# Eight accumulator banks cut by hand from one tile instead of pool buffers, in an attention and feed-forward kernel

## Chip, cores, metric

The kernel runs on one core of a Trainium2 chip. The metric is the device time of one execution in microseconds (us). In the text PE is TensorE, DVE is VectorE, ACT is ScalarE, POOL is GpSimd and SP is SyncE, which here only issues transfers.

## What is computed

Causal attention with a decay term, and a feed-forward layer on its output. There are 64 heads (batch 8 by 8) of 576 positions and 64 columns; the feed-forward layer has 4608 rows, 512 columns in and out, and 2048 columns between.

```python
scores = scale * np.matmul(q, k.transpose(0, 1, 3, 2))
cum = np.cumsum(np.maximum(s, 0.0), axis=-1)
bias = -(cum[:, :, :, None] - cum[:, :, None, :])
scores = np.where(causal, -1000000000.0, scores + np.minimum(bias, 0.0))
attn = np.exp(scores - np.max(scores, axis=-1, keepdims=True))
attn = attn / (np.sum(attn, axis=-1, keepdims=True) + 1e-09)
x = np.matmul(attn, v)          # heads side by side: (4608, 512)
h = x @ w_in                    # (4608, 2048)
g = h * np.clip(h + 3.0, 0.0, 6.0) / 6.0
out = g @ w_out                 # (4608, 512)
```

## The kernel before

**Work and tiles.** Heads go in pairs p = 0 to 31. For a pair, q and k are brought into columns: for the first ten pairs by PE transposes (`transpose_group`, L247, two groups, evacuated by DVE in the copies of L262), for later pairs by a transposing DMA (`transpose_dma`, L229) out of a staging tile `xb`. POOL fills `xb` in `cast_columns` (L222, L225, L226), with decay columns that `decay_columns` (L201 on PE, L214 and L216 on DVE) makes once.

A head's scores stand in four banks (`scores_bank`, L291 on PE). Each bank goes through an exponential on ACT (L299) and a causal mask on POOL (L304). `attend` (L340) multiplies the result by the values, and DVE divides by the row sums (L350, L352). `x_transpose` puts the result into columns, by PE (L378, copied by DVE in L386) or by a transposing DMA (L370).

The feed-forward layer runs over blocks of 512 rows. `m1` (L423) makes one of 16 pieces of h, ACT takes the relu (L431) and DVE the product (L432); `m2` (L450) makes 128 rows of the output, evacuated by DVE (L459).

**Accumulator banks.** PSUM has eight banks of 128 partitions by 512 float32. A pool holds them under four tags: "S" with three buffers (scores, PE transposes of later pairs, decay columns, some m1 pieces at the end), "M" with two (m1, some m2, early transposes), "Y" with one, and "O" with one buffer of two banks. A request for a tile of a tag gets a buffer of it, and the first writer of the new tile waits for what used the old one.

**Order.** The order of all work is written out by hand. The scheduler is off (`manual_schedule`), so each engine runs its instructions in the order of the program; `weave` lays attention tasks between the feed-forward tasks. SP issues nearly all transfers, in one queue, in program order. What the framework adds are the semaphore waits.

Of the kernel before, what the change touches and what calls it, by code (L numbers as in the profile page):

```python
# [9 lines left out]
F32 = mybir.dt.float32  # L10
F16 = mybir.dt.float16
# [5 lines left out]
def kernel(  # L17
# [30 lines left out]

    cpool = ctx.enter_context(tc.tile_pool(name="consts", bufs=1))
    work = ctx.enter_context(tc.tile_pool(name="work", bufs=2))  # L50
    psum = ctx.enter_context(tc.tile_pool(name="psum", bufs=1, space=bass.MemoryType.PSUM))

    def bank():
        return psum.tile([128, 512], F32, tag="M", bufs=2, name="bank")
# [14 lines left out]
        name="xaug",  # L69
# [527 lines left out]
    def att_tasks(p):  # L597


        more = p + 1 < NP  # L600

        def loads():
            if p + 3 < NP:
                load_qk(p + 3, nc.sync)
                load_v(p + 3, nc.sync)
            if p < PTD - 1:
                cast_qk(p + 1)

        def casts():
            if more:  # L610
                cast_v(p + 1)
            if PTD <= p + 2 < NP:
                cast_columns(p + 2)
                transpose_dma(p + 2)

        tr = [[], []]
        if p + 1 < min(NP, PTD):
            tr = [[(lambda: transpose_group(p + 1, 0), 640)],
                  [(lambda: transpose_group(p + 1, 1), 512)]]
        late = [(lambda: attend(2 * p - 1), 1200)] if p > 8 else []  # L620
        back = []
        if p > 8:
            back = [(lambda: x_transpose(p - 1), 0 if by_dma(p - 1) else 640)]
        a = [(loads, 0)]
        if p <= PXD:
            a += scores(2 * p) + tr[0] + late
            a += scores(2 * p + 1) + [(casts, 0)] + tr[1] + back
        else:
            s0, s1 = scores(2 * p), scores(2 * p + 1)
            a = late + (back + a if by_dma(p - 1) else a + s0[:2] + back)  # L630
            a += (s0 if by_dma(p - 1) else s0[2:]) + tr[0]
            a += s1 + [(casts, 0)] + tr[1]
        return a, [(lambda: attend(2 * p), 1200)]

    att_of = [[]]
    for p in range(8, NP):
        a, c = att_tasks(p)
# [124 lines left out]
```

The softmax here doesn't subtract the row's maximum and nothing guards it: scores larger than these inputs give would overflow.

## Time and profile before

| what | value |
|---|---|
| time, median of 3 runs | 375.04 us (374.9 to 375.15) |
| span of the profiled execution | 374.1 us |
| PE, busy | 354.2 us |
| ACT, busy | 209.8 us |
| DVE, busy | 190.4 us |
| POOL, busy | 149.1 us |
| HBM, over the span | 126 GB/s |

The busy time of an engine is a sum over the whole span, and matmuls overlap in the pipeline, so PE's share is not its distance from the peak. In the page's groups, the columns are: line, engine, operation, output and inputs, shape, count; then busy time and mean duration in ns; then the idle time of the engine just before these instructions and what ended it. A row of a timeline has start and length in us, engine, line, operation and count, and in brackets the idle time before it with its releaser. A row of a table of stretches has the stretch, its length, the busy time of PE, weight loads, DVE, ACT and POOL with their counts, the granted PE clock, the DMA share and GB/s.

### The profile page before, as it was taken

How to read it: one execution, taken by the hardware profiler on the slowest of the kernel's cores; microseconds unless marked ns; L12 is line 12 of the kernel's file. 1: busy time of each engine (PE TensorE's matmuls, PEld its weight loads, DVE VectorE, ACT ScalarE, POOL GpSimd, SP SyncE). 2: the span in 40 equal slices, each digit the busy share in tenths (PEclk: the TensorE clock that was granted, in tenths of full speed). 3: DMA queues.
4: the chain of work that ended last, by engine and by line, in shares of the span. 5: the costliest groups of instructions: out<-in, count | busy, mean ns of one | idle time of the engine just before them, and what ended most of it. 6: DMA issues, size and time to landing. Idle time of an engine off the chain costs nothing.

```text
span 374.1 us, 7656 instructions
## 1 busy us (share of the span) xinstructions
PE 354.2 (95%) x2805; PEld 220.5 (59%) x2805; DVE 190.4 (51%) x331; ACT 209.8 (56%) x405; POOL 149.1 (40%) x378
## 2 busy tenths in 40 slices
PE   6878879999999899999999999999999999999996
PEld 2455556556666566566656665666566655555544
DVE  5765856566642355345534553455345535554431
ACT  4464764336885677467746774677467714553310
POOL 5673344454666344444444444444444300000000
PEclk9999999999999999999999999999999999999999
DMA  9689999938899999899999989899995200011012
GB/s 162 137 155 210 205 218 204 237 108 180 157 190 197 231 172 235 188 232 198 198 208 222 206 177 234 194 196 180 213 194 112 56 31 28 28 39 46 28 58 84
DMA packets 184670, 59.36 MB, mean 159 GB/s; under 512 B 177856, under 2 KB 178336, under 8 KB 184632
## 3 DMA queue, kind: packets, MB, share of 16 engines
q1 hardware_dynamic: 182392, 54.28, 70.2%
q0 software_dynamic: 1680, 4.27, 6.4%
q8 instruction: 22, 0.36, 0.4%
q10 hardware_dynamic: 560, 0.32, 0.3%
q14 instruction: 16, 0.13, 0.1%
HBM read 37.49 MB, written 9.62 MB: 126 GB/s over the span
## 4 chain that ended last, share of the span: by engine, by line
PE 81%; DVE 5%; ACT 4%; DMA 4%; issue 2%; POOL 1%; SPq 1%; ACTq 0%; POOLq 0%
PE bank L423 26%; PE po L450 23%; PE S L291 10%; PE bank L450 7%; PE O L340 6%; PE bankS L423 4%; ACT Pm L299 3%; DMA qkT<-xb 2%; ACT trl L431 1%; DMA qkf<-in_k_dram 1%; DVE gT L432 1%; DVE qkT L262 1%; PE bank L490 1%; PE bankY L423 1%; DMA s_sb<-in_s_dram 1%
## 5 line engine op out<-in xcount | busy, mean ns | idle before, releaser
L299 ACT ACTIVATE Pm<-S 128x384 f16<-128x384 f32 (+2 forms) x256 | 115.5, 508 | 58.4 <-PE S L291 56.6
L432 DVE SCALAR_TENSOR_TENSOR gT<-trl,bank 128x512 f16<-128x512 f32 x123 | 84.5, 687 | 102.2 <-ACT trl L431 101.9
L304 POOL TENSOR_SCALAR_AFFINE_SELECT Pm<-Pm 128x128 f16<-128x128 f16 (+2 forms) x256 | 79.4, 312 | 132.7 <-ACT Pm L299 122.7
L431 ACT ACTIVATE trl<-bank,bias 128x512 f32<-128x512 f32 x123 | 85.2, 692 | 77.3 <-PE bank L423 75.5
L423 PE MATMUL bank<-xT,w_in 128*128 128x512 f16 x492 | 126.4, 382 | 0.7
L450 PE MATMUL po<-w_out_sb,gT 128*128 128x512 f16 x416 | 104.3, 379 | 0.0
L423 PEld LDWEIGHTS <-w_in 128*128 128x128 f16 x576 | 78.5, 146 | 33.3 <-issue 2.4
L450 PEld LDWEIGHTS <-gT 128*128 128x128 f16 x560 | 50.7, 98 | 46.8 <-issue 0.3
L291 PE MATMUL S<-qkT 128*128 128x320 f16 (+4 forms) x448 | 70.2, 261 | 6.8 <-ACT Pm L299 3.4
L291 PEld LDWEIGHTS <-qkT 128*128 128x128 f16 x448 | 41.0, 98 | 36.4 <-issue 3.6
L340 PEld LDWEIGHTS <-Pm 128*128 128x128 f16 x960 | 38.3, 97 | 13.4 <-POOL Pm L304 1.8
L340 PE MATMUL O<-v_h,Pm 128*128 128x65 f16 x960 | 40.8, 193 | 1.5 <-POOL Pm L304 1.3
L450 PE MATMUL bank<-w_out_sb,gT 128*128 128x512 f16 x144 | 35.8, 379 | 0.0
L352 DVE TENSOR_TENSOR xs<-O,r 128x640 f16<-128x640 f32 x32 | 26.4, 824 | 1.1
L459 DVE TENSOR_SCALAR osb<-po 128x512 f32<-128x512 f32 x26 | 17.9, 688 | 15.2 <-PE po L450 14.9
L222 POOL CAST xb<-qkf 128x1152 f16<-128x1152 f32 x22 | 25.3, 1150 | 0.0
L238 POOL CAST v_h<-v_f 128x640 f16<-128x640 f32 x28 | 20.2, 720 | 3.0 <-DMA v_f<-in_v_dram 3.0
L459 DVE TENSOR_SCALAR osb<-bank 128x512 f32<-128x512 f32 x9 | 6.2, 691 | 23.2 <-PE bank L450 23.2
L176 POOL CAST t<-qkf 128x1152 f16<-128x1152 f32 x10 | 11.5, 1154 | 13.7 <-DMA qkf<-in_k_dram 13.7
L423 PE MATMUL bankS<-xT,w_in 128*128 128x512 f16 x64 | 16.4, 379 | 0.0
L431 ACT ACTIVATE trl<-bankS,bias 128x512 f32<-128x512 f32 x16 | 11.0, 688 | 8.0 <-PE bankS L423 8.0
L432 DVE SCALAR_TENSOR_TENSOR gT<-trl,bankS 128x512 f16<-128x512 f32 x16 | 11.0, 688 | 6.8 <-ACT trl L431 6.8
(55 smaller groups left out, 130.8 us busy)
## 6 DMA issues: line engine op xcount, KB each, us to landing
qkf<-in_q_dram SPq DMA_DIRECT2D x32, 288.0 KB, 4.2
qkf<-in_k_dram SPq DMA_DIRECT2D x32, 288.0 KB, 4.3
out_dram<-osb SPq DMA_DIRECT2D x35, 256.0 KB, 2.4
v_f<-in_v_dram SPq DMA_DIRECT2D x64, 128.0 KB, 4.0
w_in<-in_moe_w_in_dram POOLq DMA_DIRECT2D x2, 1024.0 KB, 12.8
w_out_sb<-in_moe_w_out_dram POOLq DMA_DIRECT2D x4, 512.0 KB, 7.3
v_f<-in_v_dram SPq DMA_DIRECT2D x32, 32.0 KB, 2.7
qkT<-xb SPq DMA_TRANSPOSE x22, 4.9
```

The source lines that it names most:

```text
L222: nc.gpsimd.tensor_copy(out=x.rearrange("p (i t) c -> p t i c", i=2)[:, :, :, 0:D], in_=qk_f.pop(p))
L238: copy(out=v_h[:, sl, :, :, 0:D], in_=v_f[:, sl])
L291: nc.tensor.matmul(out=S[:, c:c + hi - lo], lhsT=kT[:, sl, off + 128 * kt:off + 128 * (kt + 1)], rhs=qT[:, sl, off + lo:off + hi], start=( ...
L299: nc.scalar.activation(out=P[:, p0:p0 + n], in_=S[:, 0:n], func=AF.Exp, scale=0.125, bias=0.0)
L304: nc.gpsimd.affine_select(out=view, in_=view, pattern=pattern, compare_op=ALU.is_ge, fill=0.0, base=0, channel_multiplier=-1,)
L340: nc.tensor.matmul(out=O[:, hh, qt * VW:qt * VW + D + 1], lhsT=P[:, c:c + 128], rhs=v_h[:, sl, hh, kt, 0:D + 1], start=(qt == 0), stop=(qt ...
L352: nc.vector.tensor_tensor(out=xs.rearrange("p t h d -> p h t d"), in0=Ov[:, :, :, 0:D], in1=r.to_broadcast([128, 2, 5, D]), op=ALU.mult,)
L423: nc.tensor.matmul(out=ph, lhsT=w_in_t[f // 8][:, kc, f % 8, :], rhs=xT[:, kc, n * 512:(n + 1) * 512], start=(kc == 0), stop=(kc == KC - 1),)
L431: nc.scalar.activation(out=trl, in_=ph, func=AF.Relu, bias=bias3[:, 0:1], scale=1.0)
L432: nc.vector.scalar_tensor_tensor(out=gT[n][:, f, :], in0=trl, scalar=6.0, in1=ph, op0=ALU.min, op1=ALU.mult)
L450: nc.tensor.matmul(out=po, lhsT=gT[n][:, f, t4 * 128:(t4 + 1) * 128], rhs=w_out_sb[:, f, :], start=(f == 0), stop=(f == NF - 1),)
L459: nc.vector.tensor_scalar_mul(out=osb, in0=po, scalar1=1.0 / 6.0)
```

## The change

The pool now holds one tile, `PS`, of all eight banks. A small class cuts tiles from it by hand: a counter for each tag, and the bank is the counter modulo the number of banks of the tag, so the banks of a tag are used strictly in turn. The kernel's calls stay as they are; `psum` is now this class. The framework sees one tile that lives throughout, and derives the waits from accesses to the same bank in it, instead of from the release and reuse of a buffer. It is meant to give the author the choice of the bank and to leave out the bookkeeping of buffers that are handed back.

```diff
-    psum = ctx.enter_context(tc.tile_pool(name="psum", bufs=1, space=bass.MemoryType.PSUM))
+    pspool = ctx.enter_context(tc.tile_pool(name="psum", bufs=1, space=bass.MemoryType.PSUM))
+    PS = pspool.tile([128, 8, 512], F32, tag="PS", name="PS")
+
+    class Banks:
+        first = {"S": (0, 3), "M": (3, 2), "Y": (5, 1), "O": (6, 2)}
+        n = {}
+
+        def tile(self, shape, dtype, tag, bufs=1, name=None):
+            b0, k = self.first[tag]
+            i = self.n.get(tag, 0)
+            self.n[tag] = i + 1
+            if tag == "O":
+                return PS[:, 6:8, :]
+            b = b0 + i % k
+            t = PS[:, b, :]
+            if dtype == F16:
+                t = t.bitcast(F16)
+            if len(shape) == 2:
+                return t[:, 0:shape[1]]
+            return t[:, 0:shape[1] * shape[2]].rearrange("p (a b) -> p a b", a=shape[1])
+
+    psum = Banks()
```

## The prediction

> **What bounds the kernel now.** I read the page first: engine shares, then the chain of waits, then stretches of the span, then the timeline at the places where the two programs differ.
>
> ```profile
> PE 354.2 (95%) x2805; PEld 220.5 (59%) x2805; DVE 190.4 (51%) x331; ACT 209.8 (56%) x405; POOL 149.1 (40%) x378
> ...
> PE 81%; DVE 5%; ACT 4%; DMA 4%; issue 2%; POOL 1%; SPq 1%; ACTq 0%; POOLq 0%
> ...
> L299 ACT ACTIVATE Pm<-S 128x384 f16<-128x384 f32 (+2 forms) x256 | 115.5, 508 | 58.4 <-PE S L291 56.6
> ...
> L291 PE MATMUL S<-qkT 128*128 128x320 f16 (+4 forms) x448 | 70.2, 261 | 6.8 <-ACT Pm L299 3.4
> ```
>
> TensorE (PE) is the bound; the score matmuls of L291 are the row with most idle time in front. A delay counts only if PE cannot make it up. From 127 to 309 us PE shows 181.36 us of 182 busy, so whatever is lost earlier is kept to the end. Before 127 there is one long link that is not PE:
>
> ```profile
> 92.00:93.00 1.00, 1.00 (x19) 0.76 (x18) 0.99 (x3) 0.54 (x1) 1.00 (x3) 1.00 0.00 0
> 93.00:94.00 1.00, 1.00 (x7) 0.68 (x6) 0.85 (x3) 0.32 (x2) 1.00 (x2) 1.00 0.00 0
> 94.00:95.00 1.00, 1.00 (x6) 0.64 (x6) 0.97 (x3) 0.91 (x3) 0.38 (x4) 1.00 0.00 0
> ...
> 100.00:110.00 10.00, 9.76 (x87) 6.58 (x88) 6.38 (x11) 7.68 (x16) 6.64 (x16) 1.00 1.09 195
> ...
> 94.37 2.81 SPq L229 DMA_TRANSPOSE qkT<-xb  x1
> ...
> 125.32 0.56 PE L291 MATMUL S<-qkT 128*128 128x256 f16 x4 [1.03 <-DMA qkT<-xb]
> ```
>
> The second number from the right is the DMA share: zero from 92 to 95, because SyncE's queue holds its next transfer, the transposing DMA of L229, until GpSimd (POOL) has filled xb. From 96 on the DMA engines are saturated (1.08 to 1.20) until 125.27, when the transpose issued at 119.11 lands and PE, idle for 1.03 us, goes on. So the start of that DMA burst at 94.37 sets the rest of the kernel: late by x there is late by x at the end.
>
> **What the Trainium skill says.** "TensorE: Matmul & The Clock Gate", The mechanism: matmuls are "strict FIFO" in start and end, so a matmul that waits for an older matmul of PE waits for nothing new. The trace agrees: L291 matmuls carrying such a wait start 0.216 us after a 512-column matmul and 0.056 us after a 128-column one, as matmuls without one do. "PSUM — Partial Sum Buffer", PSUM bank collisions raise a hardware error: accesses are to be guarded by semaphore per bank (and quadrant), so either kernel must make PE wait for the last reader of the same bank; what can change is which bank comes next. "Perfetto Trace Analysis", Identifying Dependency Chains: an instruction that waits on several engines may get a separate semaphore instruction ahead of it; the trace has such rows, 51 ns (median) on PE for L291 and 28 ns on SyncE for L229.
>
> **The change, part by part.** I listed both built programs, each instruction with what it waits for, and matched them to the trace by position. The order on all five engines is the same, instruction for instruction. The waits differ.
>
> (1) Self-waits of PE: 74 matmuls lose a wait for an older matmul, which a returned pool buffer brought along; 6 of them now wait for VectorE (DVE) instead, a wait that stood on their weight load before. By the pitches above the removed ones cost 0. This edit is hidden by PE's own order.
>
> (2) Six weight loads lose a DVE wait, to the matmul behind them. Where it ends last (10.44, 55.98, 72.62, 73.51 us) the weight load may now run ahead. The matmuls stood at most 0.01 us behind those loads and 0.05 us behind the release, as matmuls that wait themselves do, so I take 0; the upper bound is one load, 98 ns by its row, at four places, 0.4 us.
>
> (3) Added waits: 21 exponentials of L299 also wait for DVE, and 11 DVE copies (L262, L386) for ScalarE (ACT): the previous reader of their bank. The matmul that filled the bank already waited for that reader, so these are past when reached. Semaphore instructions go from 393 to 388 on ACT and from 57 to 68 on DVE; 11 times 28 to 51 ns is 0.3 to 0.6 us of DVE, busy for 51%, beside its wait for PE: 0 on the path. L431's waits for the older reader of trl become self-waits of ACT or go: 0.
>
> (4) Which bank comes next. The pool has not handed out the three "S" banks strictly in turn; the hand-written rotation does. At four places the next score tile gets a bank that DVE still holds.
>
> Near 46.9 us both releases (46.53, 46.63) come before the matmul starts (46.96): 0.
>
> Near 56.4 us:
>
> ```profile
> 55.98 0.72 PE L291 MATMUL S<-qkT 128*128 128x192 f16 x4 [0.55 <-DVE qkT L262]
> 57.07 0.30 PE L291 MATMUL S<-qkT 128*128 128x320 f16 x1 [0.36 <-DVE xT L386]
> ```
>
> The third bank of this head (matmuls at 56.38 and 56.52) waited for an exponential that ended at 56.33, and the fourth, at 57.07, for the xT copy of L386 that ended at 57.02. Now the third waits for the copy and the fourth for the exponential. All three matmuls start after 57.02 instead of one: the two moved ones, 0.14 and 0.03 us by their pitches, come in front of the fourth. Cost 0.17 us. Behind it stand an m1 group and the next scores; nothing up to 76 is set by DMA, so PE keeps the delay.
>
> Near 76.5 us three banks were read by the decay copies of L214. Before: the second bank started at 76.46 (exponential, 76.41), the third at 76.67, the fourth at 77.00 (copies, 76.95). Now the second may start at 76.20, the third waits for 76.95, the fourth follows it by 0.17: 77.17 against 77.00. Cost 0.17 us; the second bank's earlier start helps nobody, as ACT's next exponential still stands behind the third.
>
> Near 89.5 us, the costly one:
>
> ```profile
> 89.22 0.57 PE L291 MATMUL S<-qkT 128*128 128x192 f16 x4
> 89.63 1.06 PE L423 MATMUL bank<-xT,w_in 128*128 128x512 f16 x4
> 90.53 0.30 PE L291 MATMUL S<-qkT 128*128 128x320 f16 x1
> ...
> 89.35 0.98 DVE L262 COPY qkT<-pT 64x640 f16<-64x640 f16 x2
> ```
>
> The third bank's matmul, at 89.47 inside the first row, waited for an exponential that ended at 89.42. Now it waits for the second of the two copies in the last row, which ends at 90.33. It starts at 90.38, 0.91 us late, with nothing for PE to do meanwhile. Queued behind it on PE are the m1 group (row two) and the fourth bank (row three, now about 91.44). ACT's relu on that group, which is ahead of the fourth bank's exponential, was held by ACT's own queue for some 0.1 us, so the exponential at 91.42 slips by about 0.8. POOL's mask waits for it, then v_h, then the three copies into xb, back to back from 91.95 to 94.35, then the L229 transpose: 94.37 becomes 95.17. The saturated burst behind it passes that on to 125.32. Cost 0.8 us.
>
> Sum: 0.17 + 0.17 + 0.8 = 1.14 us. 375.04 + 1.14 = 376.2. In the steady part after 127 the pool and the rotation ask for the same readers, so nothing is added.
>
> **The rivals.** *Swallowed:* the saturated burst has some spare, or PE's short idle spots between 57 and 89 (0.3 us at 72.6, 0.4 us at 79.0) take up the 0.34 of the first two places and a part of the third. For it: PE arrives at 125.32 with 1.03 us in hand. Against: that slack is ahead of a DMA that is itself late, and DMA is empty, not busy, just before the burst. Taking half of the 1.14: 375.6. *Faster:* the self-waits or the earlier weight loads are worth more than I read. 0.4 us from the loads, and if each of the 74 waits cost even 0.02, 1.5 more, less the delay of 1.14: 374.3. Against: the pitch of the matmuls that carry them. *Much slower:* the later burst meets other traffic, and the transposes issued later in it stop PE at further score groups; twice the third place, 0.34 + 1.6: 377.0.
>
> **How the numbers follow.** Forecast 0.66, swallowed 0.17, faster 0.12, much slower 0.05. The 0.2% bound is 0.75 us, so same is 374.29 to 375.79. The forecast at 376.2 has a spread of about 0.3, so a little of it falls into same; some of the faster cases lie within 0.75. Faster 0.10, same 0.20, slower 0.70. Range 374.8 to 376.9: it takes in swallowed and most of the forecast's upper side, and leaves out the larger gain and the larger loss.
>
> **What would show it.** Right: in the profile after, an idle spot of about 0.6 us or more ahead of an L291 matmul near 90.4 us (plus 0.3), released by the qkT copy; the first L229 transpose near 95.5; PE going on after the DMA wait near 126.4; the stretch from there to the end as long as before, 248.8 us. At 57 and 77 us the waits for DVE are longer and those for ACT gone. Steps (1) to (3) are wrong if matmul pitches at the former self-waits fall below 0.216 or 0.056, or if DVE waits grow at copies. The prediction falls if the transpose starts at 94.4 as before, if PE waits less at 125, or if the part after 127 changes its length.

## The result, and the profile after

The changed kernel takes 376.71 us (median; 376.35 to 377.39), the kernel before 375.0 us (374.9 to 375.15). The ratio is 1.0043, 95% interval 1.0029 to 1.0057: slower by 1.6 us (1.1 to 2.1). The changed kernel's source has 21 lines more ahead of the body, so L291 is L312 here, L423 is L444, L262 is L283, L386 is L407, L214 is L235 and L229 is L250; all accumulator tiles are named PS.

First the page: the sums hardly moved.

```profile
PE 354.7 (95%) x2805; PEld 220.6 (59%) x2805; DVE 190.5 (51%) x331; ACT 209.8 (56%) x405; POOL 148.5 (40%) x378
...
L312 PE MATMUL PS<-qkT 128*128 128x320 f16 (+4 forms) x448 | 70.2, 261 | 7.9 <-ACT Pm L320 2.8
```

The busy time of the score matmuls is the same 70.2 us; the idle time in front of them grew from 6.8 to 7.9. A loss of this kind is not in any engine's share. Which waits end that idle time is told by PE's waits between 50 and 130 us. The kernel before:

```profile
PE S L291 <- ACT Pm L299: 1.3, 4, 0.6
...
PE S L291 <- DMA qkT<-xb: 1.0, 1, 1.0
PE S L291 <- DVE qkT L262: 0.5, 1, 0.5
...
PE S L291 <- DVE xT L386: 0.4, 1, 0.4
```

and the changed kernel, in the same stretch (total us, times, longest):

```profile
PE PS L312 <- DVE qkT L283: 1.3, 2, 0.8
...
PE PS L312 <- DVE dec L235: 0.8, 2, 0.4
PE PS L312 <- DVE xT L407: 0.7, 1, 0.7
PE PS L312 <- ACT Pm L320: 0.6, 3, 0.3
PE PS L312 <- DMA qkT<-xb: 0.6, 1, 0.6
```

Score matmuls wait 2.8 us for DVE instead of 0.9, and 0.6 for ACT instead of 1.3. The timeline of the changed kernel's PE has the three places, in order, then the matmul behind the DMA wait; the last row is SP's queue.

```profile
57.06 0.46 PE L312 MATMUL PS<-qkT 128*128 128x320 f16 x3 [0.71 <-DVE xT L407]
...
76.34 0.38 PE L312 MATMUL PS<-qkT 128*128 128x192 f16 x2 [0.42 <-DVE dec L235]
77.14 0.46 PE L312 MATMUL PS<-qkT 128*128 128x320 f16 x3 [0.42 <-DVE dec L235]
...
90.69 0.33 PE L312 MATMUL PS<-qkT 128*128 128x320 f16 x2 [0.79 <-DVE qkT L283]
90.85 1.06 PE L444 MATMUL PS<-xT,w_in 128*128 128x512 f16 x4
91.75 0.30 PE L312 MATMUL PS<-qkT 128*128 128x320 f16 x1
...
126.12 0.56 PE L312 MATMUL PS<-qkT 128*128 128x256 f16 x4 [0.57 <-DMA qkT<-xb]
...
95.50 2.82 SPq L250 DMA_TRANSPOSE qkT<-xb  x1
```

The second place in the kernel before, which the prediction gives in words only, was one row:

```profile
76.46 0.84 PE L291 MATMUL S<-qkT 128*128 128x192 f16 x5 [0.64 <-ACT Pm L299]
```

At the first two places the matmuls that used to go ahead now stand with those that wait for DVE: x3 in one row at 57.06 and 77.14. At 90.69 PE stands idle for 0.79 us and the m1 group and the fourth bank follow, 1.22 us later than before. The first transpose starts 1.13 us later. PE goes on after its DMA wait 0.80 us later (126.12 against 125.32), and its last matmul starts 0.80 us later too. The two profiles thus differ by 0.8 us where the medians differ by 1.7: a timed run takes about 1.7 us more than its span, so the profiled execution of the kernel before (span 374.1) stands for an estimated 375.8 us, more than any of that kernel's four runs.

### The profile page after: what moved, and what is told of

Read it like the earlier page. It is cut to its first block, busy times and chain, and to the rows that moved or that the text cites. A ratio compares the mean times of both kernels' runs of the same rounds, so it can differ in the third digit from the quotient of the medians.

```text
span 374.9 us, 7661 instructions
## 1 busy us (share of the span) xinstructions
PE 354.7 (95%) x2805; PEld 220.6 (59%) x2805; DVE 190.5 (51%) x331; ACT 209.8 (56%) x405; POOL 148.5 (40%) x378
## 4 chain that ended last, share of the span: by engine, by line
PE 80%; DVE 6%; DMA 5%; ACT 4%; issue 2%; POOL 1%; SPq 1%; POOLq 0%; ACTq 0%; DVEq 0%
PE PS L471 30%; PE PS L444 30%; PE PS L312 9%; PE PS L361 7%; DMA qkT<-xb 3%; ACT Pm L320 2%; ACT trl L452 1%; DVE gT L453 1%; DMA qkf<-in_k_dram 1%; DVE qkT L283 1%; PE PS L511 1%; PE PS L491 1%; PE PS L399 1%; DMA s_sb<-in_s_dram 1%; PE PS L268 1%
## 5 line engine op out<-in xcount | busy, mean ns | idle before, releaser
L453 DVE SCALAR_TENSOR_TENSOR gT<-trl,PS 128x512 f16<-128x512 f32 x144 | 98.8, 686 | 112.5 <-ACT trl L452 112.3
L452 ACT ACTIVATE trl<-PS,bias 128x512 f32<-128x512 f32 x144 | 99.5, 691 | 87.5 <-PE PS L444 85.3
L320 ACT ACTIVATE Pm<-PS 128x384 f16<-128x384 f32 (+2 forms) x256 | 115.6, 507 | 58.3 <-PE PS L312 51.5
L444 PE MATMUL PS<-xT,w_in 128*128 128x512 f16 x576 | 145.3, 381 | 0.7
L471 PE MATMUL PS<-w_out_sb,gT 128*128 128x512 f16 x560 | 139.2, 379 | 0.0
L444 PEld LDWEIGHTS <-w_in 128*128 128x128 f16 x576 | 78.4, 146 | 33.0 <-issue 2.1
L312 PE MATMUL PS<-qkT 128*128 128x320 f16 (+4 forms) x448 | 70.2, 261 | 7.9 <-ACT Pm L320 2.8
L312 PEld LDWEIGHTS <-qkT 128*128 128x128 f16 x448 | 41.1, 98 | 38.0 <-issue 5.7
L480 DVE TENSOR_SCALAR osb<-PS 128x512 f32<-128x512 f32 x35 | 24.1, 688 | 38.4 <-PE PS L471 38.1
L361 PE MATMUL PS<-v_h,Pm 128*128 128x65 f16 x960 | 40.8, 193 | 1.5 <-POOL Pm L325 1.3
L373 DVE TENSOR_TENSOR xs<-PS,r 128x640 f16<-128x640 f32 x32 | 26.4, 824 | 1.1
L283 DVE COPY qkT<-PS 64x640 f16<-64x640 f16 (+1 forms) x40 | 18.1, 453 | 5.4 <-PE PS L268 4.7
(41 smaller groups left out, 70.2 us busy)
```

The costliest lines, as they stand in the source:

```text
L283: nc.vector.tensor_copy(out=dst[0:64, sl, c0:c0 + n], in_=pT[r0:r0 + 64, 0:n])
L312: nc.tensor.matmul(out=S[:, c:c + hi - lo], lhsT=kT[:, sl, off + 128 * kt:off + 128 * (kt + 1)], rhs=qT[:, sl, off + lo:off + hi], start=( ...
L320: nc.scalar.activation(out=P[:, p0:p0 + n], in_=S[:, 0:n], func=AF.Exp, scale=0.125, bias=0.0)
L361: nc.tensor.matmul(out=O[:, hh, qt * VW:qt * VW + D + 1], lhsT=P[:, c:c + 128], rhs=v_h[:, sl, hh, kt, 0:D + 1], start=(qt == 0), stop=(qt ...
L373: nc.vector.tensor_tensor(out=xs.rearrange("p t h d -> p h t d"), in0=Ov[:, :, :, 0:D], in1=r.to_broadcast([128, 2, 5, D]), op=ALU.mult,)
L444: nc.tensor.matmul(out=ph, lhsT=w_in_t[f // 8][:, kc, f % 8, :], rhs=xT[:, kc, n * 512:(n + 1) * 512], start=(kc == 0), stop=(kc == KC - 1),)
```

## The experiments

Ratios are to the kernel before, with 95% intervals; 0.001 is 0.38 us. A profiled execution can stand early or late as a whole: the same score matmul of 55.10 us starts between 54.26 and 59.29 us in the profiles of this study, with loads in the first stage as the cause where the waits name one. So a place is read by its step, the shift behind it less the shift ahead of it, and total times from the ratios alone.

**Which of the two effects of the edit.** The edit changes the form of the waits (one tile instead of buffers) and the bank that comes next. Four kernels separate the two. With the S banks as a list of three, of which strict turn takes the oldest, the pool's own allocation differs from strict turn at four of 298 requests only. In `skip` the first number is the request, the second the place in the list that is taken instead of place 0, the oldest:

```diff
         n = {}
+        turn = [0, 1, 2]
+        skip = {37: 1, 48: 1, 72: 2, 89: 1}
...
             b = b0 + i % k
+            if tag == "S":
+                b = self.turn.pop(self.skip.get(i, 0))
+                self.turn.append(b)
```

e1_pool_choice, this edit on the changed kernel:

> Banks cut by hand from one tile, but the three S banks given out as the pool did: four requests of 298 take another bank than the oldest. Theory 'next bank' (the waits for a bank that DVE still holds make the 1.7 us): all of it goes, 375.0 us (374.8 to 375.3). Rival 'form of the waits' (one tile instead of buffers: fewer self-waits, weight loads set free, more semaphore instructions on ACT and DVE): nothing changes, 376.7.

Measured: ratio 1.000 (0.9982 to 1.0018). The waits keep their new form and the loss is gone. At 89.5 us the third bank's matmuls again stand in one row with the second's (x4, no idle time in brackets):

```profile
89.82 0.57 PE L317 MATMUL PS<-qkT 128*128 128x192 f16 x4
90.23 1.06 PE L449 MATMUL PS<-xT,w_in 128*128 128x512 f16 x4
91.13 0.30 PE L317 MATMUL PS<-qkT 128*128 128x320 f16 x1
```

e4_pool_in_turn is the opposite corner, pool buffers with the bank in turn:

```diff
...
+    class InTurn:
+        n = 0
+
+        def tile(self, shape, dtype, tag, bufs=1, name="S"):
+            if tag == "S":
+                tag, bufs = f"S{self.n % 3}", 1
+                self.n += 1
+            return pspool.tile(shape, dtype, tag=tag, bufs=bufs, name=name)
...
```

> Pool buffers as before, but S as three tags of one buffer each, asked for strictly in turn: the waits keep the form of the kernel before (self-waits and waits on weight loads), the bank that comes next is that of the changed kernel. Theory 'next bank': 376.7 (376.3 to 377.2), all of the loss. Rival 'form of the waits': 375.0.

Measured: ratio 1.0034 (1.0019 to 1.0049), 1.3 us. The loss is there without the hand-cut tile, with the same idle spot, released by the same DVE copy:

```profile
91.74 0.34 PE L302 MATMUL S<-qkT 128*128 128x320 f16 x2 [0.79 <-DVE qkT L273]
```

Its interval and that of e1 just fail to meet (1.0019 and 1.0018). The bank that comes next accounts for the loss; for the form of the waits nothing is left that these runs can tell from zero (within 0.7 us either way, so an effect of some tenths is not excluded).

**Place by place.** e2_third_as_pool has `skip = {89: 1}` (only the first two costly places in turn), e3_third_in_turn has `skip = {37: 1, 48: 1, 72: 2}` (only the third).

> As the changed kernel, but at the third place alone (89.5 us of the trace) the S bank is the one that the pool gave. Theory 'next bank': only the first two places are left, 0.34 us, so 375.3 (375.1 to 375.6), and the first L229 transpose starts 0.3 us later than in the kernel before instead of 1.13. Rival 'form of the waits': 376.7.

> As the changed kernel, but the first three places (46.9, 56.4, 76.5 us) as the pool; only at 89.5 us the bank is given in turn. Theory 'next bank': the third place alone, by the prediction 0.8 us (375.8), and up to 1.4 (376.4) if what the sum lacked is in the transfers behind it. Rival 'form of the waits': 376.7.

Measured: e2 1.0018 (1.0004 to 1.0032), 0.7 us; e3 1.0023 (1.0005 to 1.0040), 0.9 us. The two losses add up to 0.0041, the changed kernel has 0.0043; with intervals this wide the close match is in part chance. In the traces, e2 has steps of 0.16 and 0.21 us at the first two places and none at the third; e3 has none at the first two and 0.92 at the third, where PE stands idle for 0.78:

```profile
90.40 0.33 PE L317 MATMUL PS<-qkT 128*128 128x320 f16 x2 [0.78 <-DVE qkT L288]
90.57 1.07 PE L449 MATMUL PS<-xT,w_in 128*128 128x512 f16 x4
91.47 0.30 PE L317 MATMUL PS<-qkT 128*128 128x320 f16 x1
```

**Taking the DVE-held tile out of the S banks.** e10_transposes_in_y is e3 with the two transpose tiles of pair 9 in the bank of tag Y:

```diff
-        pT = half_bank(p < 4)
+        if p == 9:
+            pT = psum.tile([128, 640], F16, tag="Y", name="pTy")
+        else:
+            pT = half_bank(p < 4)
```

> As e3_third_in_turn (hand-cut banks, the first three places as the pool, strict turn from 89.5 us on), but the two transpose tiles of pair 9 stand in the bank of tag Y, which is idle from 86 to 109 us, so that no tile of the S banks is held by DVE there. Theory 'a bank held by DVE comes next': the third place costs nothing, and the waits for exponentials at 87.8 and 88.2 us (0.23 and 0.11 us of idle PE) go as well: ratio 0.999 to 1.000, PE at the fourth bank of 90.5 us 0.3 us earlier than before. Rival 'strict turn on a hand-cut tile costs there in another way': 1.0023 as e3_third_in_turn.

Measured: 0.9992 (0.9977 to 1.0007), 375.59 us beside 375.64 us of the kernel before: not told apart from it. With no DVE-held bank in the turn, strict turn on a hand-cut tile shows no cost at 89.5 us, and the waits for exponentials at 87.8 and 88.2 us go, so that in the trace the head's second bank stands 0.33 us earlier, by its step, and the fourth, expected 0.3 earlier, 0.20:

```profile
88.81 0.55 PE L320 MATMUL PS<-qkT 128*128 128x192 f16 x4
89.40 1.02 PE L452 MATMUL PS<-xT,w_in 128*128 128x512 f16 x4
90.26 0.30 PE L320 MATMUL PS<-qkT 128*128 128x320 f16 x1
```

**How a delay at 90 us reaches the end.** The prediction had the start of the DMA burst as the link. Two kernels do one m1 group of block 1 twice (0.86 us more of PE), one ahead of the burst, one inside it; e7 has `(n, f) == (1, 1)`, e8 `(1, 15)`:

```diff
-        for kc in range(KC):
+        for kc in list(range(KC)) * (2 if (n, f) == (1, 1) else 1):
```

> The kernel before, with the second m1 group of block 1 (about 87 us) done twice on PE: four more 512-column matmuls, 0.86 us, before the fourth bank at 90.5 us; the result is the same. Theory 'a delay of PE ahead of the burst is kept': the first L229 transpose 0.8 us later, the time 0.75 to 0.9 us above the kernel before (ratio 1.0022). Rival 'PE's reserve at 125 us takes it up': ratio 1.000.

> The kernel before, with the last m1 group of block 1 (108 us) done twice on PE: the same 0.86 us, but behind the start of the burst and ahead of PE's DMA wait at 125.3. Theory 'the start of the burst sets the rest': the 1.03 us that PE waits there takes it up, the wait falls to about 0.2 us, time within 0.1 us of the kernel before (ratio 1.000). Rival 'PE is the bound, every delay adds up': 0.86 us, ratio 1.0023.

Measured: e7 1.0016 (1.0007 to 1.0025), 0.6 us; e8 1.0010 (0.9994 to 1.0025), which holds both no loss and all of the 0.86. In e8's trace the shift is 0.86 us at 90.5, 1.71 behind the doubled group and 0.72 at the matmul behind the DMA wait, which has next to no idle time (0.04 us) left in front of it:

```profile
125.62 0.38 PE L450 MATMUL po<-w_out_sb,gT 128*128 128x512 f16 x1
126.04 0.34 PE L291 MATMUL S<-qkT 128*128 128x256 f16 x2
```

So in that execution, the longest of e8's ten runs, the wait for the transpose took up 0.86 us of PE, as the theory says. In e7's trace the step goes as well, against the theory: 0.54 us at 89.2 (PE's idle time at 87.8 and 88.2 hid the rest of the 0.86), 0.52 at the first transpose, 0.12 at the fourth, and 0.02 at 125.3. But this execution is the shortest of e7's 21 (374.97 us, the median is 375.92), and the ratio says that it is not the rule. The intervals of e7 and e8 overlap: that a delay ahead of the burst costs more than one inside it is not shown.

**Starting the burst earlier.** e5 (on the kernel before) and e6 (on the changed one) move one task at pair 8:

```diff
-            a += scores(2 * p) + tr[0] + late
-            a += scores(2 * p + 1) + [(casts, 0)] + tr[1] + back
+            a += [(casts, 0)] + scores(2 * p) + tr[0] + late
+            a += scores(2 * p + 1) + tr[1] + back
```

> The kernel before (pool buffers), with one task moved at pair 8: POOL casts the values and fills xb ahead of this head's masks instead of behind the next head's; PE, DVE, ACT and SP keep their order. Theory 'the start of the burst sets the rest': the first L229 transpose starts at about 90.0 us, when SP is through with its loads, instead of 94.37; PE's idle 1.03 us before 125.3 goes; the time is 1.0 us (ratio 0.9973) below the kernel before. Rival 'the burst is bound by the DMA's total, its start does not matter': the transposes still end at 125.3, ratio 1.000.

> The changed kernel (banks in turn) with the same task moved. Theory 'the start of the burst sets the rest': the fourth bank at 90.5 us is no longer on the way to the burst, but PE itself is 1.25 us later at 91 us and has no DMA wait of 1.03 us left to hide it in: 0.2 us above the kernel before (ratio 1.0006), and 1.2 us above the pool kernel with the task moved. Rival 'the third place costs through the burst alone': as the pool kernel with the task moved plus 0.34, ratio 0.998.

Measured: e5 1.0010 (0.9989 to 1.0031), e6 1.0042 (1.0027 to 1.0057). The expected gain of e5 did not come, and e6 is where the changed kernel is. SP's queue in e6 shows where the lead goes; the last row is the second transpose of xb in the kernel before:

```profile
89.83 3.02 SPq L250 DMA_TRANSPOSE qkT<-xb  x1
95.78 1.21 SPq L391 DMA_TRANSPOSE xT<-xs  x1
...
99.85 0.63 SPq L182 DMA_DIRECT2D v_f<-in_v_dram  x1
102.97 2.69 SPq L250 DMA_TRANSPOSE qkT<-xb  x1
...
102.28 2.74 SPq L229 DMA_TRANSPOSE qkT<-xb  x1
```

The first transpose starts 4.5 us earlier. The next transfer in the queue is that of L391, which waits for a result of attention, so SP is held to 95.78; and the second transpose of xb starts at 102.97, 0.7 us later than in the kernel before (102.28), because POOL fills it behind masks that hang on PE. The lead is gone at the second transpose. In e5's profile, all of which stands 4.2 us late, the first transpose leads by 4.2 us and the second by 0.2. e9 moves the task for pairs 8 to 12:

> The kernel before (pool buffers), with POOL's casts and the fills of xb ahead of the second head's masks for pairs 8 to 12 (pair 8: ahead of both heads'); PE, DVE, ACT and SP keep their order. Theory 'PE sets each transposing DMA through POOL': with all of the first ones earlier, the transpose that PE waits for at 125.3 lands earlier and the wait (1.03 us in the trace of before, 0.4 to 0.8 in the later ones) goes: ratio 0.998 to 0.999. Rival 'the DMA engines set the end of the burst': the wait stays, ratio 1.000; masks that come later may stop PE at the value matmuls, then above 1.000.

Measured: 1.0021 (0.9997 to 1.0046): no gain, and a loss that is not told apart from none. Now the transposes are early, the one of 119.11 is issued at 115.61, and the DMA wait at 125 is gone from PE's list; but the masks behind the casts are late. Of the waits between 84 and 130 us, those of PE and its weight loads for POOL:

```profile
PEld L340 <- POOL Pm L304: 3.4, 7, 0.6
...
PE O L340 <- POOL Pm L304: 1.3, 4, 0.4
```

PE's matmuls of values wait for POOL instead: 1.9 us lost between 90.5 and 123.9 in this profile, of which 1.2 come back where the kernel before waits for the DMA.

## Why the prediction was right, and where it was not

**The waits read from the two programs, steps (1) to (3): right, but for 0.04 us.** The 49 matmuls that lost a self-wait behind a 512-column matmul start 0.216 us after it (median) before and after, the 21 behind a 128-column one 0.056. Where the wait moved from the weight load to its matmul, the matmul starts 0.052 to 0.053 us after the release instead of 0.056; at 75.5 us the weight load now runs ahead and the pitch falls from 0.253 to 0.216. e1 bounds the whole at 0.7 us either way. That PE's matmuls run in order does not by itself make a wait for an older one free, since a 512-column matmul lasts 0.38 us by the profile and the next one starts after 0.216; the equal pitches show it. That the added waits on ACT and DVE were past when reached was argued from the listing; that they cost nothing measurable is in e1.

**The first two places of step (4): right.** 0.17 us each was predicted; the steps in the changed kernel's trace are 0.16 and 0.21. At 76.5 us the second bank did start earlier, and it helped nobody.

**The third place on PE, SP and POOL: right.** PE was to be 0.91 us later there; the step is 0.92 (shift 0.30 at 89.2 us, 1.22 at 90.5). The transpose was to start near 95.5: it starts at 95.50.

**"Late by x there is late by x at the end": the step that failed.** The shift of 1.13 us at the first transpose is 0.80 at 125.3 in the changed kernel's profile, and 0.86 became 0.64 in e3's. PE's wait at 125 is 0.57 us instead of 1.03, which the prediction itself had named as a sign against it. The loss of shift is in SP's queue, ahead of the fourth transpose; the kernel before, then the changed one:

```profile
116.40 1.94 SPq L157 DMA_DIRECT2D v_f<-in_v_dram  x2
119.11 3.55 SPq L229 DMA_TRANSPOSE qkT<-xb  x1
...
117.62 1.55 SPq L178 DMA_DIRECT2D v_f<-in_v_dram  x2
119.93 2.76 SPq L250 DMA_TRANSPOSE qkT<-xb  x1
```

The two loads of values hold the queue 0.39 us less in the changed kernel (whether the change has a part in that is not shown; e1, without the loss, has 1.45), and the fourth transpose is 0.82 us late where the first was 1.13. From its issue to PE's restart it is 6.2 us in both, although the transpose itself holds the queue 3.55 and 2.76 us. Nor is the burst saturated throughout, as the prediction read it: from 98 to 100 us the DMA share in the kernel before is 0.85. e5 and e6 show that an early start alone is worth nothing: each later transpose of the stage has its own way from PE over POOL, and in the kernel before the second had only 0.21 us in hand (POOL ready at 102.07, SP at 102.28). And the wait of 1.03 us, PE's reserve in the rival "swallowed", is the longest of all profiles; the others have 0 to 0.85 us there. What is kept of a delay thus differs from one profiled execution to the next.

**The sum.** 1.14 us was forecast, 1.6 (1.1 to 2.1) was measured: the forecast lies at the lower end. That it lies inside is in part luck, since the link that it rests on did not hold in the profile: the two profiles place 0.8 us of the loss only. The other 0.8 us of the loss has no place in these traces. The shares, 0.34 and 0.8 forecast, are 0.7 (0.2 to 1.2) and 0.9 (0.2 to 1.5) in e2 and e3. The trace of e2 has 0.37 us of steps at the first two places and none left at 125.3 (shift 0.11 at 55 us, 0.05 at 125.3), so its larger median is not explained by a place. The profiled execution is the shortest of e2's 21 (375.86 us, the median is 376.67); where the others lose more stays open.

**The rivals.** "Faster" fell with e1. "Swallowed" describes the single traces of e2, e7 and e8, and 0.3 us of the changed kernel's; the ratios of e4 and the changed kernel are against it, since half of the 1.14 us lies below both intervals. "Much slower", at 1.94 us, lies inside the measured interval, but has no trace: in the changed kernel and in e4 no further score group waits for a transpose behind 127 us.

## What to carry to other kernels

Writing a rotation through accumulator banks by hand had no cost here that the runs can tell from zero (within 0.7 us of 375); strict turn costs where a tile with a slow or queued reader stands in the turn, because the oldest bank is not always the first to be free. Before taking strict turn, list for each request which instruction frees its bank and when, and either skip that bank once or give the slow tile a bank outside the turn. An idle spot of 0.8 us in a span of 374 does not show in any engine's share: compare the waits by releaser.

## What was not expected

Moving POOL's work for the transposing DMAs ahead of the masks removed the DMA wait and lost more on the masks in the profile: at 40% busy, POOL was still the link between ACT and PE in this stage. And the transpose that PE waits for at 125 us took 5.8 to 6.6 us from its issue to PE's restart in the ten profiles that have this wait, whatever it held of SP's queue (2.8 to 3.55 us; the shortest of the ten goes with 3.27, the longest with 2.96). The loads of values ahead of it held the queue 1.4 to 1.9 us. Such spreads move PE's restart by several tenths of a us.
